# Gated unit of a fused attention, experts and gated-unit kernel: rows turned in squares of 32 on VectorE, sums of squares taken from the experts

## The chip, the cores and the metric

One NeuronCore of a Trainium2 chip runs the whole program. The metric is device time in microseconds (us). TensorE is called PE, VectorE DVE, ScalarE ACT, GpSimd POOL and SyncE SP, as in the profile; "the experts" is the expert layer, and "a product" is one MATMUL instruction.

## The reference, cut to what matters

Three layers follow each other. Only the last one and the rows that go into it matter here.

```python
x = _attn_ref(q, k, v)                      # 4608 rows of 512
out[mask] = gate_w[mask, None] * (np.maximum(xe @ w1[e], 0.0) @ w2[e])   # one expert of 8 per row
rms = np.sqrt(np.mean(x * x, axis=-1, keepdims=True) + 1e-06)            # gated unit, 512 -> 1536 -> 512
xn = x / rms * rms_g
g = xn @ w_gate
silu = g * (1.0 / (1.0 + np.exp(-g)))
return (silu * (xn @ w_val) @ w_out).astype(np.float32)
```

All numbers are float32; each float32 operand of a large product is split into a high and a low float32r part, so one product becomes three.

## The kernel before, in words

Attention runs first, in 36 tiles of 128 rows, and writes rows to DRAM (`x_d`). The expert layer runs in up to 25 slots of 256 rows that all belong to one expert. A slot gathers its rows, turns them on PE, multiplies with `w1` (`stage1`, L492 ff., eight steps f of 12 products with 256 columns; ACT takes the high part at L502 and DVE the low part at L503, and four PSUM tiles hold the results), then multiplies with `w2` (`stage2`, L927, two halves z of 128 rows, 24 products with 512 columns each). The result `y` lies in PSUM; ACT (z = 0, L943) or DVE (z = 1, L941) scales it with the gate into `ys`, and SP stores `ys` with one more column, the row's number, to `y_d` (L945). Half z = 1 stands under a branch (L973), since not each slot has more than 128 rows. While slots run, DVE, ACT and POOL also split the weights of the gated unit; 13 of its 18 units of weights are parked in DRAM (`scr`).

The gated unit (`NB` = 18 blocks kk of 256 rows, L1173 ff.) loads its rows with SP (`read_y`, L983), and the parked weights with POOL (`weights`, L1103). `norm` (L986) makes the steps of the normalisation: POOL copies the row numbers, ACT sums squares (L992), DVE finds 1/sqrt by Newton steps (L997 to L1007) and scales the rows (L1010). These steps are dealt out between the products of an earlier block, three behind each step c. `turn_y` (L1014) turns the rows, features to partitions, by eight transposes of 128x128 on PE (L1018); ACT takes the high part times the norm's weight (L1022) and DVE the low part (L1023). `gv(kk, c)` (L1130) is step c of 12: 24 products of 256 columns into one of three PSUM tiles `g` (L1137 to L1139), then tanh on ACT (L1141), two operations on DVE (L1142, L1143) and the split of the result into `ah`, `al` (L143, L144). `outp(kk)` (L1149) is the second multiplication: twice 36 products with 512 columns (L1158 to L1160), a copy by ACT and a scatter by POOL.

PE works in the order in which the code is written: output products of block kk-1, the eight turns for block kk+1, then the 288 products of block kk. Block 0 has its rows turned in the experts' last slot (`y0t`, in the pool of the weights); its own loop holds the turns for block 1, behind c = 9 and c = 10. The last block has no turns ahead of its products.

Tiles lie in pools in the order in which they are first asked for. The pool `g2` begins a multiple of 4096 bytes behind the first tile of the weights' pool, whose tiles all have 4096 bytes. In `g2` stand two `y` (1152 words each), two `o` (512 words) and two `gap` (8 words, L1168) ahead of `xh` and `xl`.

Of the kernel before, what the change touches and what calls it, by code (L numbers as in the profile page):

```python
# [21 lines left out]
NT = 4608  # L22
# [59 lines left out]
def fused(ctx: ExitStack, tc: tile.TileContext, q, k, v, moe_w_gate, moe_w1, moe_w2,  # L82
# [9 lines left out]
    y_d = dram.tile([NT + T, DM + 1], F32, name="y_d")  # L92
# [617 lines left out]
    nc.sync.dma_start(out=gt, in_=rms_g.rearrange("(k p o) -> p k o", p=128, o=1))  # L710
# [45 lines left out]
    ys = [mo.tile([128, DM + 1], F32, name=f"ys{i}") for i in range(2)]  # L756


    tid = sm1.tile([128, 1], I32, tag="tid", name="tid")
# [69 lines left out]
    def unit_src(u, j):  # L829
        if u < NC2:  # L830
            w = w_gate if j == 0 else w_val
            w = w.bitcast(I32) if wide else w
            n = 256 if wide else 128
            return w[:, u * n:u * n + n].rearrange("(k p) n -> p k n", p=128), 4
# [146 lines left out]
    ybl, toks = {}, {}  # L981

    def read_y(t, kk):  # L983
        nc.sync.dma_start(out=t, in_=y_d[kk * T:kk * T + T, :].rearrange("(z p) d -> p z d", p=128))

    def norm(y, tk, ms, yi, t, scratch):  # L986

        r = yi.bitcast(F32)
        steps = []

        def square(j):
            nc.scalar.activation(out=scratch(), in_=y[:, j, 0:DM], func=AF.Square, accum_out=ms[:, j:j + 1])  # L992

        steps.append(lambda: nc.gpsimd.tensor_copy(out=tk, in_=y[:, :, DM:DM + 1].bitcast(I32)))
        for j in range(2):
            steps.append(lambda j=j: square(j))
# [6 lines left out]
        for _ in range(3):  # L1003
            steps.append(lambda: nc.vector.tensor_tensor(out=t, in0=r, in1=r, op=ALU.mult))
            steps.append(lambda: nc.vector.scalar_tensor_tensor(out=t, in0=t, scalar=-0.5, in1=ms,
                                                                op0=ALU.mult, op1=ALU.mult))
            steps.append(lambda: nc.vector.scalar_tensor_tensor(out=r, in0=t, scalar=1.5, in1=r,  # L1007
                                                                op0=ALU.add, op1=ALU.mult))
        for j in range(2):
            steps.append(lambda j=j: nc.vector.tensor_scalar(  # L1010
                out=y[:, j, 0:DM], in0=y[:, j, 0:DM], scalar1=r[:, j:j + 1], scalar2=None, op0=ALU.mult))
        return steps

    def turn_y(y, to, c, px_):  # L1014
        hi, lo = to
        for d in range(2):
            for z in range(2):
                nc.tensor.transpose(px_[:, d, 128 * z:128 * z + 128],  # L1018
                                    y[:, z, (2 * c + d) * 128:(2 * c + d) * 128 + 128], ident)
# [83 lines left out]
    def weights(u):  # L1103
# [6 lines left out]
        else:  # L1110
            wo[u - NC2] = held[u]

    def load_y(kk):
# [3 lines left out]
    def norm_steps(kk):  # L1117
        toks[kk] = gs_p.tile([128, 2, 1], I32, tag="tk", bufs=3, name="tk")
        ms, yi, t = (gs_p.tile([128, 2], dt, tag=nm, name=nm) for dt, nm in ((F32, "ms"), (I32, "yi"), (F32, "t")))
        return norm(ybl[kk], toks[kk], ms, yi, t, lambda: g2.tile([128, DM], F32, tag="o", name="sq"))  # L1120

    def xpose2(kk, c):
        if c == 0:
            xts[kk] = (g2.tile([128, 4, T], F32R, tag="xh", name="xh"), g2.tile([128, 4, T], F32R, tag="xl", name="xl"))
        y = ybl[kk] if c == 0 else ybl.pop(kk)
        turn_y(y, xts[kk], c, pst.tile([128, 2, T], F32, tag=f"px{c}", name="px"))

    acts = {}

# [34 lines left out]
                in_=o, in_offset=None)  # L1164

    xts[0] = xts.pop("y0")
    load_y(1)
    g2.tile([128, 8], F32, tag="gap", name="gap")  # L1168
    for c in range(NC2):
        weights(c)  # L1170
    for c in range(6):
        weights(NC2 + c)
    for kk in range(NB):  # L1173


        todo = [] if kk else norm_steps(1)
        if kk:
            outp(kk - 1)
            if kk + 1 < NB:
                xpose2(kk + 1, 0)  # L1180
                xpose2(kk + 1, 1)
            if kk + 2 < NB:
                load_y(kk + 2)
                todo = norm_steps(kk + 2)
        for c in range(NC2):
            gv(kk, c)
            if kk:
                for f in todo[3 * (c - 5):3 * (c - 4)] if c > 4 else ():
                    f()
                continue  # L1190
            for f in todo[3 * (c - 2):3 * (c - 1)] if c > 1 else ():
                f()
            if c in (9, 10):
                xpose2(1, c - 9)
            if c == 8:
                load_y(2)
            if c == 11:
                for f in norm_steps(2):
                    f()
    outp(NB - 1)  # L1200


# [29 lines left out]
```

## Time and profile before

| | us |
|---|---|
| three runs, median (lowest to highest) | 1722.82 (1719.47 to 1733.78) |
| the profiled execution | 1731.15 |
| span of its instructions | 1729.1 |
| first to last product of the gated unit's first multiplication | 798.3 to 1705.9 |

The profiled execution is longer than the median and inside the spread of the runs. The profile's page gives the busy time of each engine; its views by window, by line, by time and by waits are cut to the rows below. A product in the time view begins where PE starts it; its written duration overlaps that of the next ones, so the distance of starts is what PE needs for one.

### The profile page before, as it was taken

What the parts mean: (1) busy time and instruction counts of PE and PEld (TensorE: products, weight loads), DVE (VectorE), ACT (ScalarE), POOL (GpSimd) and SP (SyncE); (2) the same over time, 40 slices, a digit from 0 to 9 for tenths busy, and PEclk for the clock granted to TensorE, in tenths of its full rate; (3) what the DMA queues carried; (4) which work ended last, traced back from release to release, by engine and by line L of the source; (5) the groups of instructions that cost most, each with busy time, mean ns of one, the idle gap of its engine ahead of it and who ended that gap; (6) DMA issues with size and microseconds to landing.
All of it is one profiled execution on the core that took longest, in us unless ns stands there. A gap on an engine that the chain in (4) does not pass through costs nothing.

```text
span 1729.1 us, 31214 instructions
## 1 busy us (share of the span) xinstructions
PE 1640.8 (95%) x11373; PEld 1507.4 (87%) x11373; DVE 883.4 (51%) x2087; ACT 527.8 (31%) x1202; POOL 425.9 (25%) x469
## 2 busy tenths in 40 slices
PE   7897888999899999998999999999999999999998
PEld 5897877878788888888899999999999999999997
DVE  5787875588866688423434433333433333443322
ACT  2344442244524244222222222222222222222221
POOL 4665564355534555212100000000000000000000
PEclk7798889999999999999999999999999999999999
DMA  9889665456754664214600000000000000000000
GB/s 183 220 167 189 127 110 157 132 194 226 258 191 148 200 210 142 75 51 169 217 10 19 23 26 25 25 26 7 20 25 25 25 25 7 20 26 13 13 13 13
DMA packets 111632, 162.16 MB, mean 94 GB/s; under 512 B 46032, under 2 KB 65616, under 8 KB 111456
## 3 DMA queue, kind: packets, MB, share of 16 engines
q1 hardware_dynamic: 99744, 124.03, 26.7%
q0 software_dynamic: 11712, 35.91, 6.1%
q8 instruction: 94, 1.54, 0.4%
q14 instruction: 82, 0.67, 0.1%
HBM read 116.85 MB, written 43.06 MB: 92 GB/s over the span
## 4 chain that ended last, share of the span: by engine, by line
PE 50%; DMA 2%; issue 1%; POOL 0%; POOLq 0%; ACT 0%
PE g L1138 11%; PE g L1139 11%; PE g L1137 11%; PE po L1159 6%; PE po L1160 6%; PE po L1158 6%; DMA rl<-scr 1%; PE px L1018 1%; DMA rh<-scr 1%; DMA out_dram<-o,tk 0%; POOL rh L1107 0%; POOL rl L1107 0%; POOLq L1226 0%; ACT o L1161 0%; POOLq L1107 0%
## 5 line engine op out<-in xcount | busy, mean ns | idle before, releaser
L1138 PE MATMUL g<-xl,rh 128*128 128x256 f32 x1088 | 302.8, 278 | 0.0
L1139 PE MATMUL g<-xh,rl 128*128 128x256 f32 x1088 | 302.7, 278 | 0.0
L1137 PE MATMUL g<-xh,rh 128*128 128x256 f32 x1088 | 302.4, 278 | 0.0
L1162 POOL DMA_INDIRECT out_dram<-o,tk x36 | 34.7, 965 | 793.9 <-ACT o L1161 708.4
L1138 PEld LDWEIGHTS g<-xl,rh 128*128 128x128 f32 x1088 | 204.3, 188 | 0.0
L1137 PEld LDWEIGHTS g<-xh,rh 128*128 128x128 f32 x1088 | 204.1, 188 | 0.0
L1139 PEld LDWEIGHTS g<-xh,rl 128*128 128x128 f32 x1088 | 204.0, 187 | 0.0
L498 PE MATMUL p<-xh,w1h 128*128 128x256 f32 x672 | 191.6, 285 | 7.7 <-DVE hl L503 7.1
L499 PE MATMUL p<-xl,w1h 128*128 128x256 f32 x672 | 190.0, 283 | 1.9 <-DVE xl L535 1.9
L500 PE MATMUL p<-xh,w1l 128*128 128x256 f32 x672 | 189.6, 282 | 0.0
L1142 DVE SCALAR_TENSOR_TENSOR th<-th,g 128x256 f32<-128x256 f32 x216 | 90.9, 421 | 191.8 <-ACT th L1141 191.3
L1023 DVE SCALAR_TENSOR_TENSOR xl<-px,gt,xh 128x256 fp32r<-128x256 f32 x68 | 31.4, 482 | 265.3 <-ACT xh L1022 265.3
L1137 PE MATMUL g<-xh,uh 128*128 128x256 f32 x544 | 152.6, 280 | 0.0
L1138 PE MATMUL g<-xl,uh 128*128 128x256 f32 x544 | 151.4, 278 | 0.0
L1139 PE MATMUL g<-xh,ul 128*128 128x256 f32 x544 | 151.4, 278 | 0.0
L143 ACT CAST ah<-th 128x256 fp32r<-128x256 f32 x216 | 88.0, 407 | 203.4 <-DVE th L1143 203.4
L1141 ACT ACTIVATE th<-g 128x256 f32<-128x256 f32 x216 | 82.6, 382 | 206.7 <-PE g L1139 206.6
L144 DVE TENSOR_TENSOR al<-th,ah 128x256 fp32r<-128x256 f32 x216 | 91.9, 425 | 102.2 <-ACT ah L143 102.2
L1159 PE MATMUL po<-rl,ah 128*128 128x512 f32 x360 | 142.4, 395 | 1.5 <-DMA rl<-scr 1.5
L1158 PE MATMUL po<-rh,ah 128*128 128x512 f32 x360 | 142.3, 395 | 0.0
L1160 PE MATMUL po<-rh,al 128*128 128x512 f32 x360 | 142.2, 395 | 0.0
L498 PEld LDWEIGHTS p<-xh,w1h 128*128 128x128 f32 x672 | 127.6, 190 | 12.3 <-DVE hl L503 8.3
(263 smaller groups left out, 3641.6 us busy)
## 6 DMA issues: line engine op xcount, KB each, us to landing
st<-in_moe_w_dram SPq DMA_DIRECT2D x64, 512.0 KB
y_d<-ys SPq DMA_DIRECT2D x39, 256.5 KB
y<-y_d SPq DMA_DIRECT2D x18, 513.0 KB
v<-in_v_dram SPq DMA_DIRECT2D x32, 288.0 KB
x_d<-x SPq DMA_DIRECT2D x32, 260.0 KB
q<-in_q_dram SPq DMA_DIRECT2D x32, 256.0 KB
scr<-uh SPq DMA_DIRECT2D x13, 512.0 KB
scr<-ul SPq DMA_DIRECT2D x13, 512.0 KB
```

Of the source, the lines that this page charges most:

```text
L143: nc.scalar.copy(out=hi, in_=src)
L144: eng.tensor_tensor(out=lo, in0=src, in1=hi, op=ALU.subtract)
L498: nc.tensor.matmul(a, lhsT=w1h[d][:, fs], rhs=xh[:, d], start=d == 0, stop=False)
L499: nc.tensor.matmul(a, lhsT=w1h[d][:, fs], rhs=xl[:, d], start=False, stop=False)
L500: nc.tensor.matmul(a, lhsT=w1l[d][:, fs], rhs=xh[:, d], start=False, stop=d == 3)
L1137: nc.tensor.matmul(g[:, j], lhsT=wh[:, sl], rhs=hi[:, d], start=d == 0, stop=False)
L1138: nc.tensor.matmul(g[:, j], lhsT=wh[:, sl], rhs=lo[:, d], start=False, stop=False)
L1139: nc.tensor.matmul(g[:, j], lhsT=wl[:, sl], rhs=hi[:, d], start=False, stop=d == 3)
L1142: nc.vector.scalar_tensor_tensor(out=th, in0=th, scalar=1.0, in1=g[:, 0], op0=ALU.add, op1=ALU.mult)
L1158: nc.tensor.matmul(po, lhsT=ah[:, tsl], rhs=wh[:, sl], start=c == 0, stop=False)
L1159: nc.tensor.matmul(po, lhsT=ah[:, tsl], rhs=wl[:, sl], start=False, stop=False)
L1160: nc.tensor.matmul(po, lhsT=al[:, tsl], rhs=wh[:, sl], start=False, stop=c == NC2 - 1)
```

## The change

Every row's sum of squares is taken in the experts: after `ys` is scaled, ACT squares `y` in place with the gate as scale and adds it up into a further column of `ys`; `y_d` gets that column. In the gated unit the rows of a block come in by four DMAs of 32 partitions (each 8 x 128 words per partition, so that squares of 32x32 lie where they are to be turned), their sums by four more and the row numbers by one. DVE scales the rows, turns them in two STREAM_TRANSPOSE instructions, and ACT and DVE split the result from SBUF. Features are numbered so that partition p holds features 4p to 4p+3; the loads of `w_gate`, `w_val` and `rms_g` and the turns of block 0 follow that. PE's eight turns go; one transpose of the constant identity stands in their place ahead of each block from 1 to 17. The tile `gap` goes and `y` has 1024 words; `yt` (one buffer of 1024 words) stands between `y` and `xh`.

```diff
+        nc.scalar.activation(out=y, in_=y, func=AF.Square, scale=g, accum_out=ys[z][:, DM + 1:DM + 2])
         r = nc.values_load(row_i[START:START + 1, s:s + 1], engines=(ET.SP,), min_val=0, max_val=NT)
         nc.sync.dma_start(out=y_d[bass.ds(r + 128 * z, 128), :], in_=ys[z])
...
     def load_y(kk):
-        ybl[kk] = g2.tile([128, 1152], F32, tag="y", name="y")[:, 0:2 * DM + 2].rearrange("p (z d) -> p z d", z=2)
-        read_y(ybl[kk], kk)
+        ybl[kk] = g2.tile([128, 8, 128], F32, tag="y", name="y")
+        sq[kk] = gs_p.tile([128, 8], F32, tag="sq", bufs=2, name="sq")
         toks[kk] = gs_p.tile([128, 2, 1], I32, tag="tk", bufs=3, name="tk")
+        rows = y_d[kk * T:kk * T + T, :]
+        for a in range(4):
+            ps_ = slice(32 * a, 32 * a + 32)
+            nc.sync.dma_start(out=ybl[kk][ps_], in_=rows[:, 128 * a:128 * a + 128].rearrange("(b i) d -> i b d", i=32))
+            nc.sync.dma_start(out=sq[kk][ps_].unsqueeze(2),
+                              in_=rows[:, DM + 1:DM + 2].rearrange("(b i) d -> i b d", i=32))
+        nc.sync.dma_start(out=toks[kk].bitcast(F32), in_=rows[:, DM:DM + 1].rearrange("(z p) d -> p z d", p=128))
+    def turn_steps(kk):
+        y, ms = ybl.pop(kk), sq.pop(kk)
+        steps = newton(ms, yi, t)
+        yt = g2.tile([128, 4, T], F32, tag="yt", bufs=1, name="yt")
+        xts[kk] = hi, lo = tuple(g2.tile([128, 4, T], F32R, tag=nm, name=nm) for nm in ("xh", "xl"))
+        def scale(h):
+            b = slice(4 * h, 4 * h + 4)
+            nc.vector.tensor_tensor(out=y[:, b], in0=y[:, b], in1=r[:, b].unsqueeze(2).to_broadcast([128, 4, 128]),
+                                    op=ALU.mult)
+        def turn(h):
+            c = slice(2 * h, 2 * h + 2)
+            nc.vector.transpose(out=yt[:, c].rearrange("p c (b i) -> p c b i", i=32),
+                                in_=y.rearrange("p b (j c) -> p c b j", c=4)[:, c])
+        def part(c):
+            nc.scalar.activation(out=hi[:, c], in_=yt[:, c], func=AF.Copy, scale=gt[:, c])
+            nc.vector.scalar_tensor_tensor(out=lo[:, c], in0=yt[:, c], scalar=gt[:, c], in1=hi[:, c],
+                                           op0=ALU.mult, op1=ALU.subtract)
+        return (steps + [lambda h=h: scale(h) for h in range(2)] + [lambda h=h: turn(h) for h in range(2)] +
+                [lambda c=c: part(c) for c in range(4)])
...
+    turned = pst.tile([128, 128], F32, tag="px", name="turned")
     load_y(1)
-    g2.tile([128, 8], F32, tag="gap", name="gap")
...
+        todo = turn_steps(kk + 1) if kk + 1 < NB else []
         if kk:
             outp(kk - 1)
-            if kk + 1 < NB:
-                xpose2(kk + 1, 0)
-                xpose2(kk + 1, 1)
-            if kk + 2 < NB:
-                load_y(kk + 2)
-                todo = norm_steps(kk + 2)
+            nc.tensor.transpose(turned, ident, ident)
+        if kk + 2 < NB:
+            load_y(kk + 2)
         for c in range(NC2):
             gv(kk, c)
+            for f in todo[2 * c:2 * c + 2] if kk else todo[3 * (c - 5):3 * (c - 4)] if c > 4 else ():
                 f()
```

On PE, between the output products (`po`) of block 0 and the products (`g`) of block 1, the kernel before has:

```order
L1160 MATMUL po<-uh_9334,al 128x512
L1018 MATMUL px<-cc,y 128x128 x8
L1137 MATMUL g<-xh,uh_2948 128x256
L1138 MATMUL g<-xl,uh_2948 128x256
L1139 MATMUL g<-xh,ul_2949 128x256
```

and the changed kernel has:

```order
L1196 MATMUL po<-uh_9368,al 128x512
L1215 MATMUL turned<-cc 128x128
L1173 MATMUL g<-xh,uh_2948 128x256
L1174 MATMUL g<-xl,uh_2948 128x256
L1175 MATMUL g<-xh,ul_2949 128x256
```

Eight turns of data have become one turn of constants (`cc`), and nothing else moved on PE at this place.

On SP, behind the store of the last slot (`ys` to `y_d`) and the ends of the slots' branches, the kernel before has the 17 loads of rows:

```order
L945 DMA y_d<-ys_2941 128x513
L973 UNCONDITIONAL_BRANCH x2
L1082 UNCONDITIONAL_BRANCH x7
L984 DMA y<-y_d 128x2x513 x17
```

and the changed kernel has nine for each block, of which the first block's stand here:

```order
L947 DMA y_d<-ys_2941 128x514
L975 UNCONDITIONAL_BRANCH x2
L1091 UNCONDITIONAL_BRANCH x7
L1133 DMA y<-y_d 32x8x128
L1134 DMA sq<-y_d 32x8x1
L1133 DMA y<-y_d 32x8x128
L1134 DMA sq<-y_d 32x8x1
L1133 DMA y<-y_d 32x8x128
L1134 DMA sq<-y_d 32x8x1
L1133 DMA y<-y_d 32x8x128
L1134 DMA sq<-y_d 32x8x1
L1136 DMA tk<-y_d 128x2x1
```

A load of 256 pieces has become nine loads of 2304 pieces: 1024 of 512 bytes and 1280 of 4 bytes.

On ACT, at the end of a slot of the experts (`ys_2940` belongs to the half z = 0, `ys_2941` to z = 1 inside its branch, `hh` to the next slot's first products), the changed kernel has:

```order
L944 ACTIVATE ys_2940<-y,gates 128x512
L945 ACTIVATE y,ys_2940<-y,gates 128x512
L883 CAST uh_4378<-ub 128x512
L907 TENSOR_LOAD row_i
L975 COMPARE_AND_BRANCH
L945 ACTIVATE y,ys_2941<-y,gates 128x512
L975 UNCONDITIONAL_BRANCH x2
L503 ACTIVATE hh<-p_0_3228 128x256
```

where the kernel before has

```order
L943 ACTIVATE ys_2940<-y,gates 128x512
L882 CAST uh_4370<-ub 128x512
L906 TENSOR_LOAD row_i
L973 COMPARE_AND_BRANCH
L973 UNCONDITIONAL_BRANCH x2
L502 ACTIVATE hh<-p_0_3226 128x256
```

Both squares are new; that of z = 1 stands ahead of the next slot's first `hh` and behind DVE's use of the same `y`.

## Rows read from the trace of the kernel before

**Rows 1.** Window of one block: length, PE, PEld, DVE, ACT, POOL busy (instructions), granted clock, DMA, GB/s.
```profile
1570.20:1621.80 51.60, 51.60 (x370) 48.29 (x369) 19.43 (x54) 13.48 (x34) 2.11 (x3) 1.00 0.03 11
```

**Rows 2.** Time view of PE: last output product and first two products, around eight turns.
```profile
1569.87 0.40 PE L1160 MATMUL po<-uh,al 128*128 128x512 f32 x1
...
1570.90 0.36 PE L1137 MATMUL g<-xh,uh 128*128 128x256 f32 x1
1571.10 0.28 PE L1138 MATMUL g<-xl,uh 128*128 128x256 f32 x1
```

**Rows 3.** Time view of PE: the same at block 17, which has no turns.
```profile
1671.78 0.39 PE L1160 MATMUL po<-uh,al 128*128 128x512 f32 x1
1672.01 0.28 PE L1137 MATMUL g<-xh,uh 128*128 128x256 f32 x1
1672.12 0.28 PE L1138 MATMUL g<-xl,uh 128*128 128x256 f32 x1
```

**Rows 4.** Chain that ended last: turns ahead of blocks 1, 10, 11 and 12.
```profile
854.33 0.87 PE px L1018 x8
...
1314.85 0.87 PE px L1018 x8
1365.16 0.87 PE px L1018 x8
...
1416.76 0.87 PE px L1018 x8
```

**Rows 5.** Time view of PE: block 10, block 17: its 288 products' start or end.
```profile
1315.48 0.36 PE L1137 MATMUL g<-xh,uh 128*128 128x256 f32 x1
...
1348.20 0.39 PE L1158 MATMUL po<-rh,ah 128*128 128x512 f32 x1
...
1705.93 0.40 PE L1158 MATMUL po<-rh,ah 128*128 128x512 f32 x1
```

**Rows 6.** Time view of PE: block 0, first product of c = 2 and turns behind c = 9.
```profile
805.49 0.28 PE L1137 MATMUL g<-y0t,uh 128*128 128x256 f32 x1
...
828.53 0.60 PE L1018 MATMUL px<-cc,y 128*128 128x128 f32 x4
```

**Rows 7.** Time view of PE: experts' slot 0, two products twelve apart.
```profile
260.18 0.28 PE L499 MATMUL p<-xt,w1h 128*128 128x256 f32 x1
...
261.62 0.28 PE L499 MATMUL p<-xt,w1h 128*128 128x256 f32 x1
```

**Rows 8.** Groups by line on DVE and ACT: busy, mean ns | idle before, releaser.
```profile
L426 DVE TENSOR_TENSOR x<-av,rs 128x512 f32<-128x512 f32 x35 | 23.8, 680 | 0.0
...
L992 ACT ACTIVATION_READ_ACCUMULATOR sq<-y 128x1 f32 x36 | 6.7, 187 | 0.0
L943 ACT ACTIVATE ys<-y,gates 128x512 f32<-128x512 f32 x22 | 15.1, 686 | 32.8 <-PE y L935 22.8 <-PEq L973 3.6 <-ACTq L910 2.5
L941 DVE TENSOR_SCALAR ys<-y,gates 128x512 f32<-128x512 f32 x17 | 12.7, 748 | 42.8 <-PE y L935 41.7 <-DMA st<-in_moe_w_dram 1.1
```

**Rows 9.** Time view of all engines at the end of a slot of the experts.
```profile
602.94 0.75 DVE L941 TENSOR_SCALAR ys<-y,gates 128x512 f32<-128x512 f32 x1 [4.06 <-PE y L935]
...
604.42 0.38 ACT L502 ACTIVATE hh<-p 128x256 fp32r<-128x256 f32 x1 [5.84 <-PE p L500]
...
606.26 0.42 DVE L503 SCALAR_TENSOR_TENSOR hl<-p,hh 128x256 fp32r<-128x256 f32 x1 [0.99 <-ACT hh L502]
```

**Rows 10.** DMA queues in 804:812 (two), 14:17 and 84.3:84.7: packets, MB, share of 16 engines.
```profile
q0 software_dynamic: 498, 1.84, 64.1%
q1 hardware_dynamic: 544, 1.05, 40.2%
...
q1 hardware_dynamic: 1607, 0.57, 100.5%
...
q0 software_dynamic: 28, 0.00, 5.1%
```

**Rows 11.** Chain that ended last: the last parked weights.
```profile
836.00 7.05 DMA rl<-scr
```

More of the change, by code (lines that the diff above doesn't have):

```diff
@@ L91, in fused @@
     x_d = dram.tile([NT, XW], F32, name="x_d")
-    y_d = dram.tile([NT + T, DM + 1], F32, name="y_d")
+    y_d = dram.tile([NT + T, DM + 2], F32, name="y_d")
     ord_d = dram.tile([E * NT, 1], I32, name="ord_d")
@@ L709, in fused @@
     nc.sync.dma_start(out=ct, in_=cst[:, C_TRI:C_END])
-    nc.sync.dma_start(out=gt, in_=rms_g.rearrange("(k p o) -> p k o", p=128, o=1))
+    nc.sync.dma_start(out=gt, in_=rms_g.rearrange("(p k o) -> p k o", k=4, o=1))
     nc.sync.dma_start(out=ord_d.rearrange("(p n) o -> p (n o)", p=128), in_=bigt)
@@ L755, in fused @@
     xgs = [mo.tile([128, 2, XW], F32, name=f"xg{i}") for i in range(2)]
-    ys = [mo.tile([128, DM + 1], F32, name=f"ys{i}") for i in range(2)]
+    ys = [mo.tile([128, DM + 2], F32, name=f"ys{i}") for i in range(2)]
     tid = sm1.tile([128, 1], I32, tag="tid", name="tid")
@@ L833, in unit_src @@
             n = 256 if wide else 128
-            return w[:, u * n:u * n + n].rearrange("(k p) n -> p k n", p=128), 4
+            return w[:, u * n:u * n + n].rearrange("(p k) n -> p k n", k=4), 4
         w = w_out.bitcast(I32) if wide else w_out
@@ L983, in read_y, with newton @@
     def read_y(t, kk):
-        nc.sync.dma_start(out=t, in_=y_d[kk * T:kk * T + T, :].rearrange("(z p) d -> p z d", p=128))
-    def norm(y, tk, ms, yi, t, scratch):
+        nc.sync.dma_start(out=t, in_=y_d[kk * T:kk * T + T, 0:DM + 1].rearrange("(z p) d -> p z d", p=128))
+    def newton(ms, yi, t):
         r = yi.bitcast(F32)
         steps = []
[L991 to L996, printed above, removed]
         steps.append(lambda: nc.vector.tensor_scalar(out=ms, in0=ms, scalar1=1.0 / DM, scalar2=1e-6,
@@ L1008, in norm, with square @@
                                                                 op0=ALU.add, op1=ALU.mult))
+        return steps
+    def norm(y, tk, ms, yi, t, scratch):
+        steps = []
+        def square(j):
+            nc.scalar.activation(out=scratch(), in_=y[:, j, 0:DM], func=AF.Square, accum_out=ms[:, j:j + 1])
+        steps.append(lambda: nc.gpsimd.tensor_copy(out=tk, in_=y[:, :, DM:DM + 1].bitcast(I32)))
+        for j in range(2):
+            steps.append(lambda j=j: square(j))
+        steps += newton(ms, yi, t)
+        r = yi.bitcast(F32)
         for j in range(2):
@@ L1018, in turn_y @@
                 nc.tensor.transpose(px_[:, d, 128 * z:128 * z + 128],
-                                    y[:, z, (2 * c + d) * 128:(2 * c + d) * 128 + 128], ident)
+                                    y[:, z, 2 * c + d:DM:4], ident)
         for d in range(2):
@@ L1111, in weights @@
             wo[u - NC2] = held[u]
+    sq = {}
     def load_y(kk):
-        ybl[kk] = g2.tile([128, 1152], F32, tag="y", name="y")[:, 0:2 * DM + 2].rearrange("p (z d) -> p z d", z=2)
-        read_y(ybl[kk], kk)
-    def norm_steps(kk):
+        ybl[kk] = g2.tile([128, 8, 128], F32, tag="y", name="y")
+        sq[kk] = gs_p.tile([128, 8], F32, tag="sq", bufs=2, name="sq")
         toks[kk] = gs_p.tile([128, 2, 1], I32, tag="tk", bufs=3, name="tk")
-        ms, yi, t = (gs_p.tile([128, 2], dt, tag=nm, name=nm) for dt, nm in ((F32, "ms"), (I32, "yi"), (F32, "t")))
-        return norm(ybl[kk], toks[kk], ms, yi, t, lambda: g2.tile([128, DM], F32, tag="o", name="sq"))
@@ L1122, in xpose2 @@
[L1122 to L1126, printed above, removed]
+        rows = y_d[kk * T:kk * T + T, :]
[4 more added lines that the diff above has]
+                              in_=rows[:, DM + 1:DM + 2].rearrange("(b i) d -> i b d", i=32))
@@ new lines, in load_y @@
+        nc.sync.dma_start(out=toks[kk].bitcast(F32), in_=rows[:, DM:DM + 1].rearrange("(z p) d -> p z d", p=128))
+    def turn_steps(kk):
+        y, ms = ybl.pop(kk), sq.pop(kk)
+        yi, t = (gs_p.tile([128, 8], dt, tag=nm, name=nm) for dt, nm in ((I32, "yi"), (F32, "t")))
+        steps = newton(ms, yi, t)
+        r = yi.bitcast(F32)
+        yt = g2.tile([128, 4, T], F32, tag="yt", bufs=1, name="yt")
[14 more added lines that the diff above has]
+                [lambda c=c: part(c) for c in range(4)])
@@ L1173, in fused @@
     for kk in range(NB):
-        todo = [] if kk else norm_steps(1)
+        todo = turn_steps(kk + 1) if kk + 1 < NB else []
         if kk:
             outp(kk - 1)
-            if kk + 1 < NB:
-                xpose2(kk + 1, 0)
-                xpose2(kk + 1, 1)
-            if kk + 2 < NB:
-                load_y(kk + 2)
-                todo = norm_steps(kk + 2)
+            nc.tensor.transpose(turned, ident, ident)
+        if kk + 2 < NB:
+            load_y(kk + 2)
         for c in range(NC2):
             gv(kk, c)
[L1187 to L1191, printed above, removed]
-                f()
[L1193 to L1199, printed above, removed]
+            for f in todo[2 * c:2 * c + 2] if kk else todo[3 * (c - 5):3 * (c - 4)] if c > 4 else ():
+                f()
     outp(NB - 1)
```

## The prediction, made before the changed kernel had run

> **What bounds the kernel now.** I looked at the window view by stage first, then at the time view of PE, then at what shares the other engines and the DMA queues. From block 1 to the end PE works without a gap: in one block of 51.60 us its busy time is 51.60, while DVE has 19.43 and ACT 13.48 [rows 1], at the full 2.4 GHz (granted clock 1.00). So in this half of the program only what PE itself starts costs time; work that moves to DVE or ACT is free as long as no wait for it reaches PE. In a block PE starts 288 products of 256 columns, 72 output products of 512 and eight turns.
>
> The reader should see next that blocks differ. The turns ahead of blocks 10, 11 and 12 begin 50.31 and 51.60 us apart; from block 1 to block 10 it is 460.52, three times 50.31 + 51.60 + 51.60 within 0.01 [rows 4]. So every third block (1, 4, ... 16) is 1.29 us shorter. Block 10, a short one, takes 32.72 us for its 288 products, 113.6 ns each [rows 5]; a long block then takes 32.72 + 1.29 = 34.01, 118 ns each; block 17 takes 1705.93 - 1672.01 = 33.92, the long kind, and is the one block with no turns ahead of it [rows 3, 5]. Block 0 is a third kind: 192 products in 23.04 us, 120.0 ns each [rows 6]. The experts' slot 0 has the same 120.0 (twelve products in 1.44 us) [rows 7]. Nothing waits in any of these: PE's own rhythm differs by 6%, and with 17 blocks of 288 products that is more time than the turns themselves.
>
> **The turns on PE.** With eight turns the distance from the last output product to the second product is 1571.10 - 1569.87 = 1.23 us [rows 2]; with none it is 1672.12 - 1671.78 = 0.34 [rows 3]. Eight turns so cost 0.89, one about 0.11, and one is left: 0.78 saved for each of blocks 1 to 16, less 0.11 for block 17, which gains a turn: 16 x 0.78 - 0.11 = 12.4 us. Block 0 loses its own eight turns, 0.9 us, but behind block 0 PE waits for the last parked weights, which land at 843.05 [rows 11]; I count nothing for them.
>
> **The place of the moving operand.** The two tiles that are read at 120.0 ns (`y0t`, `xt`) lie in the weights' pool. In pool `g2`, `xh` stands 2 x 4608 + 2 x 2048 + 2 x 32 = 13,376 bytes behind the pool's beginning, 64 bytes past a multiple of 512; the beginning itself is a multiple of 4096 bytes from every weight tile and from `y0t` and `xt`. After the change `y` takes 2 x 4096 and `yt` 4096, `gap` is gone, and `xh` and `xl` stand at multiples of 4096 from `y0t`. So every block's moving operand gets the place that in this trace always ran at 120.0 ns, at several starts: straight, behind four turns of block 0, and in slot 0 of the experts. That the place is the cause is my reading of three cases that agree, not something the trace isolates. By it a block's products take 288 x 0.1200 + 0.08 (the first one behind a turn) = 34.64 us: 1.92 more in six short blocks, 0.63 more in ten long ones, 0.72 in block 17, together 11.5 + 6.3 + 0.7 = 18.5 us lost. The bounds from the nearest rows are the other two rhythms: all 17 blocks at 32.72 would give back 10 x 1.29 + 1.20 = 14.1; all at 34.01 would lose 6 x 1.29 = 7.7. I take +18.5, the row with the same place.
>
> The Trainium skill says otherwise: in "TensorE: Matmul & The Clock Gate", "Step-by-step: what each phase is for", the gap between products in a stream is the number of columns in cycles plus about 2.5 ns, by which 256 columns would take about 109 ns (an estimate from that page) wherever they lie. The trace has 113.6, 118 and 120.0, so here the rule gives a floor and no single rhythm; by it this term would be 0.
>
> **DVE and ACT in a block.** Two turns by DVE are shown by no row. The nearest of 512 elements are L426's 680 ns and L941's 748 [rows 8]; between none and three times the latter a pair costs 0 to 4.5 us, and I take 1.4. The scaling with a broadcast operand is priced as L426: 2 x 0.68. DVE's 19.43 us becomes about 22, ACT loses two squares. All lies beside 50 us of PE. Three `g` tiles give two steps of c (5.7 us) before a late DVE stops PE, so even 4.5 costs nothing.
>
> **Experts.** A square is priced as L943's 686 ns from the same PSUM tile plus 187 for reading the sum: 0.87 us, 22 + 17 times [rows 8], 34 us of ACT. For z = 0 it lies beside the other half's 24 products. For z = 1 it waits for DVE: DVE ends at 603.69, the square at about 604.6, where ACT took the next `hh` at 604.42; behind it DVE idled 0.99 us [rows 9], which absorbs 0.2 to 0.5. SP's store comes 0.9 later at a point where only later slots' loads queue behind it. Bounds: nothing, and 17 x 0.5 = 8 us; no gain, since work is only added. I take 1, near the idle row.
>
> **The first block's loads.** Both loads of rows run beside the parked weights. A packet of 2052 bytes took 0.402 x 16 x 8 us / 544 = 95 ns; packets of mostly 256 bytes 1.005 x 16 x 3 / 1607 = 30 ns; packets of 4 bytes 0.051 x 16 x 0.4 / 28 = 12 ns [rows 10]. A load becomes 1024 x 0.037 (an estimate between 30 and 95, nearer the first) + 1280 x 0.012 = 53 us over 16 engines, 3.3 us, against 256 x 0.095 / 16 = 1.5. Two loads add 3.6 us to a stream whose end PE waits for [rows 11]. I take 3; bounds 0 (if they fit ahead of the weights) and 8 (below).
>
> **Sum.** -12.4 + 18.5 + 1 + 3 = +10.1 us. The profiled execution would go from 1731.15 to 1741; it lies 8.3 above the median of the runs, so from that median of 1722.8 I forecast 1733.
>
> **Rivals.**
> 1. The one turn puts every block in the short rhythm. For it: only blocks behind turns ever had it, and block 17 did not. Against it: block 0 has turns in its middle and stays at 120.0 on both sides. -12.4 - 14.1 + 4 = -22.5: 1700.
> 2. The rhythms stay as a mix (-12.4 + 4: 1714), or all blocks have the long one (-12.4 + 7.7 + 4: 1722), because the place is not the cause. For it: 118 ns is the commonest kind.
> 3. Slower: DVE is held in block 0. Its first Newton step stands behind step c = 5 and needs the four loads of sums, the last of which is eighth in SP's row; DVE's work for c = 6 is queued behind it. PE fills three `g` tiles and must stop at 828.53 - 2.88 = 825.65. DVE then needs 1.4 us to free one, so this decides from a landing later than 824.2 on. In the shared window the two queues passed 498 and 544 packets, about one for one [rows 10]. One for one with 4096-byte packets, 2048 small ones last 128 per engine x 0.2 = 26 us from 804, to 830 to 832. PE stops for 6 to 8 us instead of 3 for this term: forecast + 5, and 8 more if the weights behind slip too: 1738 to 1746. The Trainium skill bears on it: "DMA: Bandwidth & Descriptors", "Queues, rings and completion order", says that each engine takes turns between queues packet by packet, and that a packet can hold many descriptors; by the latter the small ones would pass faster than I count, and 498 to 544 agrees with the first half of the rule only.
>
> **How the numbers follow.** Chances: forecast 0.42 (own range 1726 to 1741), rival 1 0.28, rival 2 0.18, rival 3 0.12. A measurement of this kernel tells about 1%, 17 us, from no change: faster means under 1706, slower over 1740. Faster: nine tenths of rival 1 and a little of rival 2, 0.26. Slower: rival 3 (0.12) and 0.03 of the forecast's case, 0.15. The rest, 0.59, is no change. Cases of both signs hold the chance, so the range runs from rival 1's 1700 less 1 to 1743, the middle of rival 3.
>
> **What would show it.** Right: 288 products of a block in 34.6 us in all blocks; 0.46 us from the last output product to the second product; DVE near 22 us in a block with no PE idle; PE's wait for `rl` behind block 0 a few us longer. Wrong: any block at 32.7 or 34.0 (the place is not the cause), PE idle in block 0 with DVE at its first Newton step (rival 3), PE idle at slot ends behind ACT's square.

## The result, and the profile after

The changed kernel took 1735.68 us (median of 20 runs, 1727.78 to 1747.33), the kernel before 1724.42 beside it (20 runs, 1719.47 to 1733.78). The ratio is 1.0058, with a 95% interval from 1.0042 to 1.0073: a little slower, by less than the 1% from which the prediction's chances count a change. The forecast was 1733.

The profiled execution took 1731.95 us and its span is 1730.1, against 1731.15 and 1729.1 before. The two spans are 1 us apart and the medians 11, so the spans must not be subtracted. The attention and the experts ahead of the gated unit took anything from 789 to 809 us in the profiled executions of this study, whatever the edit. I therefore count each trace from block 0's first product:

| | before | after | difference |
|---|---|---|---|
| first product of block 0 | 798.26 | 789.25 | (spread of executions) |
| from there to block 1's first product | 56.70 | 67.07 | +10.4 |
| from there to the last output product | 867.54 | 867.19 | -0.4 |

All of the loss lies in block 0, and the 17 blocks behind it come out even. The window view shows block 0 of the kernel before; its columns are those of [rows 1]:

```profile
798.26:854.96 56.70, 55.19 (x377) 51.01 (x377) 22.27 (x68) 14.72 (x39) 15.19 (x29) 0.97 0.79 274
```

and block 0 and a later block of the kernel after:

```profile
789.25:856.29 67.04, 58.67 (x360) 54.13 (x361) 21.44 (x56) 11.38 (x29) 14.93 (x27) 0.87 1.14 232
...
1570.81:1621.84 51.03, 51.03 (x364) 48.15 (x363) 21.30 (x56) 12.06 (x30) 1.92 (x2) 1.00 0.03 11
```

In the later block PE is busy for the whole 51.03 us at full clock, as in [rows 1], and DVE's time went from 19.43 to 21.30. In block 0 PE is idle for 8.4 us (1.5 before), and the granted clock is 0.87 (0.97 before): part of it runs at the lower of the clock's two levels.

The time view of PE in a later block answers to [rows 2, 3, 5]:

```profile
1570.43 0.40 PE L1196 MATMUL po<-uh,al 128*128 128x512 f32 x1
1570.66 0.27 PE L1215 MATMUL turned<-cc 128*128 128x128 f32 x1
1570.69 0.36 PE L1173 MATMUL g<-xh,uh 128*128 128x256 f32 x1
1570.89 0.28 PE L1174 MATMUL g<-xl,uh 128*128 128x256 f32 x1
...
1605.33 0.40 PE L1194 MATMUL po<-rh,ah 128*128 128x512 f32 x1
...
1621.45 0.40 PE L1196 MATMUL po<-uh,al 128*128 128x512 f32 x1
```

Three things are to be read. From the last output product to the second product it is 0.46 us (1.23 before). The 288 products take 1605.33 - 1570.69 = 34.64 us, 120.0 ns each, and so they do in all 17 blocks. And the 72 output products take 1621.45 - 1605.33 = 16.12 us from the first to the last start, 227 ns each; before it was 16.56, 233 ns each: in block 10 from 1348.20 [rows 5] to

```profile
1364.76 0.40 PE L1160 MATMUL po<-uh,al 128*128 128x512 f32 x1
```

This third one I had not looked at.

The groups by line on DVE and ACT, the columns those of [rows 8]:

```profile
L1153 DVE STREAM_TRANSPOSE yt<-y 128x512 f32<-128x512 f32 x34 | 36.4, 1107 | 0.0
L1148 DVE TENSOR_TENSOR y<-y,yi 128x512 f32<-128x512 f32 x34 | 21.9, 684 | 0.0
L992 DVE TENSOR_SCALAR sq<-sq 128x8 f32<-128x8 f32 x17 | 2.8, 165 | 9.4 <-DMA sq<-y_d 9.4
...
L945 ACT ACTIVATE y<-y,gates 128x512 f32<-128x512 f32 x39 | 25.6, 656 | 55.2 <-issue 28.7 <-DVE ys L942 24.0 <-DMA st<-in_moe_w_dram 2.5
```

A turn of 512 elements per partition takes DVE 1107 ns; a pair is 2.2 us (I took 1.4, bounds 0 to 4.5). L992 is the first Newton step: over all 17 blocks DVE waited 9.4 us for the sums, and the time views of DVE and of PE show that all of it stands in block 0:

```profile
810.50 0.42 DVE L145 TENSOR_TENSOR al<-th,ah 128x256 fp32r<-128x256 f32 x1 [0.47 <-ACT ah L144]
820.29 0.17 DVE L992 TENSOR_SCALAR sq<-sq 128x8 f32<-128x8 f32 x1 [9.36 <-DMA sq<-y_d]
...
821.23 0.42 DVE L1179 SCALAR_TENSOR_TENSOR th<-th,g 128x256 f32<-128x256 f32 x1
```

```profile
816.99 0.28 PE L1175 MATMUL g<-y0t,rl 128*128 128x256 f32 x1
821.70 0.58 PE L1173 MATMUL g<-y0t,rh 128*128 128x256 f32 x1 [4.43 <-DVE th L1179]
822.08 0.42 PE L1174 MATMUL g<-y0t,rh 128*128 128x256 f32 x1
```

DVE is held from 810.93 to 820.29 by the landing of the sums. PE fills its three `g` tiles, starts its last product at 816.99 and goes on at 821.70, when the first tile comes free: 4.6 us lost. Then it runs at the lower clock for a while, as the window view of the stop and of the stretch behind it shows:

```profile
816.99:821.70 4.71, 0.28 (x3) 0.08 (x2) 1.26 (x5) 0.02 (x1) 1.59 (x3) 0.90 1.75 362
821.70:827.62 5.92, 5.92 (x27) 5.92 (x28) 4.01 (x16) 2.09 (x6) 1.06 (x2) 0.50 1.64 350
```

27 products take 5.92 us at a granted clock of 0.50, the 1.2 GHz level, where 27 x 0.12 is 3.24: 2.7 us more, 7.3 in all.

Why the sums come late: the eight loads of rows and sums of block 1 are issued by SP from 794.00 on, and in the window 794 to 820 the DMA queues passed, by packets, MB and share of 16 engines:

```profile
q0 software_dynamic: 2162, 7.91, 97.1%
q1 hardware_dynamic: 2337, 0.53, 57.7%
```

q0 has the parked weights, q1 the rows: one packet for one, and some 2300 packets, one block's load, need 26 us. From 800 to 833, in each single microsecond, the numbers of packets that the two queues begin lie within 6 of each other (72 to 107 each).

The chain that ended last, in block 0 (start, us, what), answers to [rows 11]:

```profile
812.74 12.36 DMA rh<-scr
825.15 8.19 issue
833.35 0.47 POOL rh L1116
833.87 9.29 DMA rl<-scr
843.20 0.80 PE po L1195
844.00 0.43 PE po L1196
```

At 825.15 the last pair of parked weights waits for the tile it is to go into. It is the one of `y0t`, and POOL's wait ends with the last product of block 0 ("PE g L1175" in the time view of POOL). So block 0's products set when that pair is issued, and the pair sets when the output products of block 0 can be finished. Counted from block 0's first product, the last load is issued after 44.6 us (before: 37.7), lands after 53.9 (44.8), and block 1 starts after 67.1 (56.7). The 10.4 us are thus 6.9 of a later issue (DVE's hold, passed on), 2.2 of a longer transfer and 1.3 behind it, where output products run at the lower clock for 5 us (843.2 to 848.2: granted clock 0.51, 0.43 us apart; 1.00 in the kernel before) and the eight turns are gone.

### The profile page after: what moved, and what is told of

Same layout as the page of the kernel before. It is cut to its first block, busy times and chain, and to the rows that moved or that the text cites. A ratio compares the mean times of both kernels' runs of the same rounds, so it can differ in the third digit from the quotient of the medians.

```text
span 1730.1 us, 31209 instructions
## 1 busy us (share of the span) xinstructions
PE 1634.9 (94%) x11253; PEld 1508.3 (87%) x11254; DVE 916.5 (53%) x2121; ACT 529.0 (31%) x1212; POOL 423.8 (24%) x452
## 4 chain that ended last, share of the span: by engine, by line
PE 50%; DMA 2%; issue 1%; POOL 0%; POOLq 0%; ACT 0%
PE g L1175 11%; PE g L1174 11%; PE g L1173 11%; PE po L1195 5%; PE po L1196 5%; PE po L1194 5%; DMA rl<-scr 1%; DMA rh<-scr 1%; DMA out_dram<-o,tk 0%; POOL rh L1116 0%; PE turned L1215 0%; POOL rl L1116 0%; POOLq L1248 0%; ACT o L1197 0%; POOLq L1116 0%
## 5 line engine op out<-in xcount | busy, mean ns | idle before, releaser
L1173 PE MATMUL g<-xh,rh 128*128 128x256 f32 x1088 | 307.9, 283 | 0.0
L1174 PE MATMUL g<-xl,rh 128*128 128x256 f32 x1088 | 307.9, 283 | 0.0
L1175 PE MATMUL g<-xh,rl 128*128 128x256 f32 x1088 | 307.9, 283 | 0.0
L1173 PEld LDWEIGHTS g<-xh,rh 128*128 128x128 f32 x1088 | 208.9, 192 | 0.0
L1174 PEld LDWEIGHTS g<-xl,rh 128*128 128x128 f32 x1088 | 208.9, 192 | 0.0
L1175 PEld LDWEIGHTS g<-xh,rl 128*128 128x128 f32 x1088 | 208.9, 192 | 0.0
L1175 PE MATMUL g<-xh,ul 128*128 128x256 f32 x544 | 154.0, 283 | 0.0
L500 PEld LDWEIGHTS p<-xl,w1h 128*128 128x128 f32 x672 | 129.4, 193 | 2.5 <-DVE xl L536 1.8
```

Of the source, the lines that this page charges most:

```text
L500: nc.tensor.matmul(a, lhsT=w1h[d][:, fs], rhs=xl[:, d], start=False, stop=False)
L1173: nc.tensor.matmul(g[:, j], lhsT=wh[:, sl], rhs=hi[:, d], start=d == 0, stop=False)
L1174: nc.tensor.matmul(g[:, j], lhsT=wh[:, sl], rhs=lo[:, d], start=False, stop=False)
L1175: nc.tensor.matmul(g[:, j], lhsT=wl[:, sl], rhs=hi[:, d], start=False, stop=d == 3)
```

## The experiments

Byte places below are those of the tiles in a partition, in the compiled program, modulo 512. All weight tiles, `y0t` among them, stand at 448. The kernels ran in groups, each group on one chip beside the kernel before, whose median differs by up to 8 us from group to group; so I compare ratios to it.

**e1_gap: the gap put back.** `xh`, `xl`, `ah` and `al` stand at 0 again, as before the change, and nothing else differs.

```diff
     load_y(1)
+    g2.tile([128, 8], F32, tag="gap", name="gap")
```

> The changed kernel with the 64 bytes of the old gap put back ahead of yt, xh, xl, o, ah and al; all else as changed. Place theory (where the moving operand lies sets the distance of products): no block from 1 to 17 stays at 120.0 ns; they go to 113.3 or 117.8, and output products, whose stationary operand moves by 64 bytes too, go from about 226.5 back to 233.3 ns. Time against the changed kernel: 17 blocks lose between 0.63 and 1.92 us of products and gain 0.48 us of output products, so -2.5 to -24 us. Rival (the turns between output and next products set the distance, not the place): 120.0 ns stays and the time is that of the changed kernel, 1736, within 2.

Measured: ratio 1.0057 (1.0030 to 1.0083). In its trace all 17 blocks have 117.8 ns a product, 34.01 us, and output products take 16.57 us again:

```profile
1318.33 0.36 PE L1173 MATMUL g<-xh,uh 128*128 128x256 f32 x1
...
1352.33 0.39 PE L1194 MATMUL po<-rh,ah 128*128 128x512 f32 x1
...
1368.90 0.39 PE L1196 MATMUL po<-uh,al 128*128 128x512 f32 x1
```

So the place moves both rhythms, in opposite directions: 0.63 us won and 0.45 lost per block, 3 us in 17 blocks, which is too little for the ratio to show. The short rhythm of 113.3 does not come with one turn at this place.

**e2_before_nogap: the kernel before without its gap**, with eight turns of data as ever.

```diff
     load_y(1)
-    g2.tile([128, 8], F32, tag="gap", name="gap")
```

> The kernel before with its gap of 64 bytes taken out and nothing else changed, so eight turns of data stand between output and next products. Place theory: all blocks at 120.0 ns, block period 34.56 + 0.9 of turns + 72 output products; +18.5 us of products, and -8 us if output products go to 226.5 ns because ah moves by the same 64 bytes: 1724 + 10 = 1735. Rival (turns set the distance): mix of 113.3 and 117.8 stays, time 1724 within 2.

Measured: 1.0100 (1.0054 to 1.0147; four runs). All 17 blocks are at 120.0 ns, their outputs at 16.12 us. Block 10 takes 34.64 us:

```profile
1316.77 0.36 PE L1137 MATMUL g<-xh,uh 128*128 128x256 f32 x1
...
1351.41 0.40 PE L1158 MATMUL po<-rh,ah 128*128 128x512 f32 x1
```

The mix of 113.3 and 117.8 is gone although turns, squares and loads are those of the kernel before. The 64 bytes alone make the 120.0; that it is the place of `xh` and `xl` and not of `ah` and `al` is for the next run to show.

**e3_swap_gap: the two places apart.** Pool `ga` stands ahead of `g2`, so `ah` keeps 448 while the gap brings `xh` to 0.

```diff
-    g2 = gctx.enter_context(tc.tile_pool(name="g2", bufs=2))
     ga = gctx.enter_context(tc.tile_pool(name="ga", bufs=13))
+    g2 = gctx.enter_context(tc.tile_pool(name="g2", bufs=2))
...
     load_y(1)
+    g2.tile([128, 8], F32, tag="gap", name="gap")
```

> As e1_gap, but the pool of ah and al stands ahead of that of y, yt, xh and xl, so only xh and xl (and yt, o) move by 64 bytes and ah, al keep the place mod 512 of the changed kernel. If the two places act one by one: products as in e1_gap (113.3 or 117.8 ns) and output products at about 226.5 ns, 17 x 0.48 = 8 us less than e1_gap. If it is one place for both (the sum of all that moves): the same as e1_gap.

Measured: 1.0002 (0.9977 to 1.0026). The two places act one by one: 34.01 us for the products and 16.12 for the outputs in every block. In the time view of block 10:

```profile
1317.94 0.36 PE L1173 MATMUL g<-xh,uh 128*128 128x256 f32 x1
...
1351.95 0.39 PE L1194 MATMUL po<-rh,ah 128*128 128x512 f32 x1
...
1368.07 0.40 PE L1196 MATMUL po<-uh,al 128*128 128x512 f32 x1
```

**e4_noturn: no turn of constants.**

```diff
-    turned = pst.tile([128, 128], F32, tag="px", name="turned")
...
-            nc.tensor.transpose(turned, ident, ident)
```

> The changed kernel without the one turn of constants. If the turn only costs what it takes: 17 x 0.11 to 0.2 us less, -2 to -3.5 us, products stay at 120.0 ns. Rival (the turn sets the rhythm): the distance of products changes from 120.0 ns, and the time by several us either way.

Measured: 1.0052 (1.0025 to 1.0080). 120.0 ns stay; a block's period is 50.90 us instead of 51.03. At place 448 the turn sets no rhythm and costs 0.13 us per block, 2.2 in all.

**e5_late0: block 1's steps later**, so that DVE does not wait for the sums ahead of block 0's own work.

```diff
-            for f in todo[2 * c:2 * c + 2] if kk else todo[3 * (c - 5):3 * (c - 4)] if c > 4 else ():
+            for f in todo[2 * c:2 * c + 2] if kk else todo if c == 11 else ():
```

> The changed kernel with one edit: in block 0 all of block 1's steps (Newton, scaling, turns, splits) stand behind step c = 11 instead of three behind each step from c = 5 on. Theory (DVE's hold): in the changed kernel's trace PE stops 7.3 us at c = 8 to 10 of block 0, because DVE waits 9.4 us for the sums and the g tiles fill; the last parked weights wait for block 0's last products (their tile is the one of y0t), so the hold is passed on whole. With the edit block 0 takes 34.6 us for its 288 products instead of 41.9, the last parked weights are issued some 37 us behind block 0's first product instead of 44, and block 1 begins 58 to 60 us behind it instead of 67: 7 to 9 us off the time, 1725 to 1729. Rival (the transfer sets the end): the parked weights, slowed by the small packets of the rows' loads, land as late as before, PE waits at the output products for what it no longer waits for in the products: gain 0 to 2 us, 1733 to 1736. Second rival (the late steps become late themselves): block 1 waits for its xh, gain lost.

Measured: 1.0044 (1.0009 to 1.0078); the changed kernel's 1.0058 lies inside this interval. The trace says more. Block 0's products take 37.34 us instead of 43.75 and no wait for DVE is left among them; the last load is issued 38.2 us behind the first product instead of 44.6; but it then takes longer:

```profile
844.24 2.56 issue
...
847.33 11.83 DMA rl<-scr
```

11.83 us instead of 9.29, and block 1 starts after 62.5 us instead of 67.1. The first two expectations each had a part: the hold is removed, 6.4 us, and 2.5 are given back to the transfer. What runs beside it is seen in the queues: between 847 and 859 q1 still passed 2396 packets, the rows of block 2 and, issued by SP from 854.67 on, those of block 3.

**e7_late0_y1: as e5, with one `y` tile**, so that the rows of blocks 2 and 3 cannot be loaded beside the parked weights.

```diff
-        ybl[kk] = g2.tile([128, 8, 128], F32, tag="y", name="y")
+        ybl[kk] = g2.tile([128, 8, 128], F32, tag="y", bufs=1, name="y")
```

> As the kernel with block 1's steps behind c = 11, and one y tile instead of two, so that the load of rows for block 2 waits until block 1's rows are turned, and every later load likewise: one load of 2304 pieces, not two, shares block 0's time with the parked weights. xh, xl, ah and al keep their places mod 512 bytes. If the small pieces slow the weights: the parked weights that are issued early pass faster (the issues of the 13 pairs end some 2 to 3 us earlier against block 0's first product), the last pair lands 7 us behind its issue instead of 9.3, and the time is 1 to 3 us under that of the kernel with two y tiles. If it is the products of block 0 that hold the last pair: the same time within 1 us. Against both, one y tile could make a later block wait for its rows: then PE idles in blocks 1 to 16 and the time is over 1736.

Measured: 1.0004 (0.9979 to 1.0029).

```profile
843.41 8.74 DMA rl<-scr
```

The last load takes 8.74 us (I had expected 7), block 1 starts 56.9 us behind block 0's first product (56.7 in the kernel before), and no later block waits for its rows. The 5.6 us won against e5 are more than the 1 to 3 that I expected: 3.1 are the transfer, 0.9 its earlier issue, and 1.6 the output products behind it, which here run at full clock from the landing on (granted clock 1.00 from 852.2 to 863.0). While the last weights land (843 to 852), the queues passed

```profile
q0 software_dynamic: 855, 3.10, 98.4%
q1 hardware_dynamic: 37, 0.02, 3.1%
```

where in the changed kernel (834 to 843, SP issuing the rows of block 3 from 834.54 on) they had passed

```profile
q1 hardware_dynamic: 2952, 0.64, 68.1%
q0 software_dynamic: 324, 1.15, 64.4%
```

e5 and e7 move like amounts of weights (852 and 855 packets of q0), so the 3.1 us between their transfers are the small packets' price; in the changed kernel only 324 packets of weights were left, since the hold had let the earlier pairs land, and they took 9.29 us all the same. That accounts for block 0: a hold of DVE by the small packets of block 1's rows, and a slower last transfer by those of blocks 2 and 3.

**e6_square2: the experts' squares doubled**, to price their term.

```diff
+        nc.scalar.activation(out=y, in_=y, func=AF.Copy, accum_out=ys[z][:, DM + 1:DM + 2])
         nc.scalar.activation(out=y, in_=y, func=AF.Square, scale=g, accum_out=ys[z][:, DM + 1:DM + 2])
```

> The changed kernel with a second pass of ACT over y (a copy in place with a sum, 0.66 + 0.19 us) ahead of each square in the experts, so the added work on ACT is doubled: 22 + 17 times 0.85 us, 33 us of ACT. Theory (the predicted idle time hides the square): one square per half fits into slack, since the spans of the experts are alike without and with it (first to last scaling of the second half 488.3 us before, 485.8 after); of the second, the half under the branch stands between DVE's scaling and the next slot's first hh, and 0.5 to 0.85 us per slot come through in up to 17 slots: 8 to 14 us in the experts' span, 1744 to 1750. Rival (ACT in the experts is far off PE's path, so squares cost nothing at any number): 1733 to 1738 with the experts' span unchanged. Rival (the first square already costs its 0.5 per slot and something else hid it): the second costs its whole 0.85 x 17 = 14 us.

Measured: 1.0058 (1.0037 to 1.0078), the ratio of the changed kernel itself. The theory fell: 39 more passes of 0.59 + 0.19 us, 30 us of ACT, cost nothing that can be measured (the interval is some 3.5 us to either side). From the first to the last scaling of a second half the experts take 491.7 us; traces with one square have 483.2 to 491.6, the two without (the kernel before and e2) 488.3 and 488.7. In the slot end that I followed, ACT's passes end at 582.6; ACT has two `hh` ready at once behind them and then waits 0.81 us for PE, so the delay is caught up in the next slot's first steps.

**e8_eight: as e3_swap_gap, with eight turns of constants.**

```diff
-            nc.tensor.transpose(turned, ident, ident)
+            for _ in range(8):
+                nc.tensor.transpose(turned, ident, ident)
```

> The changed kernel with pool ga ahead of g2 and a tile of 64 bytes, so that xh stands at a multiple of 512 bytes and ah 64 bytes ahead of one, and eight turns of the constant identity ahead of each block instead of one. The same with one turn took 1725.8 with all blocks at 117.8 ns a product. If the turns set the rhythm at this place: every third block (or every block) goes at 113.6 ns, 1.29 us less in 6 blocks (or 1.2 in 17), and seven more turns cost 7 x 0.11 x 17 = 13 us: 1731 (or 1718). If what they move matters (data from y, with ACT and DVE taking px), not their number: all blocks at 117.8 and 13 us more, 1738 to 1740.

Measured: 1.0077 (1.0036 to 1.0118), 0.0075 above e3_swap_gap, 12.9 us: seven turns more in 17 blocks at 0.11 each. All blocks stay at 117.8. Eight turns alone do not bring back the short rhythm of the kernel before.

**e9_scan_a and e10_scan_b: other places and numbers of turns.** On top of e3, e5 and e7, `xh` and `xl` of odd and of even blocks have places of their own, and the number of turns changes every four blocks. The gap has 32 words in e9 and 48 in e10.

```diff
+        if kk == 2:
+            g2.tile([128, 32], F32, tag="gap2", bufs=1, name="gap2")
-        xts[kk] = hi, lo = tuple(g2.tile([128, 4, T], F32R, tag=nm, name=nm) for nm in ("xh", "xl"))
+        xts[kk] = hi, lo = tuple(g2.tile([128, 4, T], F32R, tag=f"{nm}{kk % 2}", bufs=1, name=f"{nm}{kk % 2}")
+                                 for nm in ("xh", "xl"))
...
+    g2.tile([128, 32], F32, tag="gap", bufs=1, name="gap")
...
-            nc.tensor.transpose(turned, ident, ident)
+            for _ in range((1, 8, 0, 3)[min((kk - 1) // 4, 3)]):
+                nc.tensor.transpose(turned, ident, ident)
```

> Pool ga ahead of g2, one y tile, block 1's steps behind c = 11, as in the kernel of the same call without a scan; and the moving operand of blocks of odd number at 64 mod 512 bytes, of even number at 192, with 1, 8, 0 and 3 turns of constants ahead of blocks 1 to 4, 5 to 8, 9 to 12 and 13 to 17. So far 448 mod 512 (the weights' own) gave 120.0 ns a product, 0 gave 117.8 or 113.3. Theory (place alone): each parity has one rhythm in all its blocks, whatever the turns; 64 and 192, being off the weights' place, have 117.8 or 113.3. Rival (the number of turns chooses between 113.3 and 117.8 where the place is off the weights'): the rhythm changes at blocks 5, 9 or 13, in both parities. Second rival (only the weights' place is special): 117.8 in all 17 blocks.

> The same with odd blocks at 128 and even blocks at 256 mod 512 bytes. Theory (place alone): one rhythm for each parity. Rival (turns): a change at blocks 5, 9 or 13. Second rival: 117.8 in all 17 blocks.

Measured, one run each: 1731.45 and 1719.16 us, where the kernel before had 1732.26. The reading is the rhythm of each block. With those of the other runs (ns per product):

| place of `xh`, `xl` | behind 1 or 8 turns | behind 0 or 3 turns |
|---|---|---|
| 0 (e1, e3, e8, e11) | 117.8 | 117.8 (0 turns: block 17 of the kernel before) |
| 64 (odd blocks of e9) | 118.7 | 120.0 |
| 128 (odd blocks of e10; e12) | 113.3 | 117.8 |
| 192 (even blocks of e9) | 120.0 | 120.0 |
| 256 (even blocks of e10) | 117.8 | 117.8 |
| 448 (after, e2, e4) | 120.0 | 120.0 (0 turns) |

The theory that only the weights' place is special fell, and so did that of the place alone: at 128 the number of turns chooses (and not the block's number: e12 below has one turn ahead of blocks 9 to 17 too, and 113.3 in them). In the time view of e10_scan_b, block 5 (eight turns) and block 9 (none), first product and first output product of each:

```profile
1055.69 0.37 PE L1176 MATMUL g<-xh,uh 128*128 128x256 f32 x1
...
1088.42 0.39 PE L1197 MATMUL po<-rh,ah 128*128 128x512 f32 x1
...
1256.94 0.28 PE L1176 MATMUL g<-xh,uh 128*128 128x256 f32 x1
...
1290.86 0.39 PE L1197 MATMUL po<-rh,ah 128*128 128x512 f32 x1
```

32.73 us against 33.92, in blocks with the same tiles at the same place.

**e11_best1: what the runs gave, together**: e3's order of pools and gap, e5's late steps, e7's one `y` tile.

> The changed kernel with what the runs so far gave: pool ga ahead of g2 and a tile of 64 bytes (xh at 0 mod 512, ah at the weights' place), one y tile, block 1's steps behind c = 11. From its own terms: 17 blocks with 288 products at 117.8 instead of 120.0 ns, 10.7 us less, and block 0 with 57 us instead of 67 to the start of block 1, 10 us less; the changed kernel stood 1.0058 of the kernel before, so 1.0058 - 20.7 / 1725 = 0.994. If the two edits hide each other (they are at different blocks, so they should not): 0.997 to 1.000.

Measured: 1718.05 us, 0.9918 (0.9893 to 0.9944). The two edits add up: in its trace blocks 1 to 17 take 10.8 us less than in the changed kernel and block 0 takes 9.7 less. It is faster than the kernel before and the changed one.

**e12_all128: the same with `xh`, `xl` at 128 in all blocks.**

```diff
-    g2.tile([128, 8], F32, tag="gap", name="gap")
+    g2.tile([128, 48], F32, tag="gap", bufs=1, name="gap")
```

> As e11_best1, which took 0.9918 of the kernel before with all blocks at 117.8 ns a product and xh at 0 mod 512 bytes; here xh and xl stand at 128 mod 512 in all blocks, with one turn of constants. In the scan, odd blocks at 128 ran at 113.3 with one turn or eight, and at 117.8 with none or three, each behind an even block at 256. If a block's rhythm follows from its own place and the number of turns: 113.3 in all 17 blocks, 1.28 us less in each, 21.8 us, 0.979. If it follows from the point in PE's rhythm at which the block ahead left off as well: some blocks at 113.3 (a third, as in the kernel before, would give 0.987; half 0.985), or none (0.992).

Measured: 1697.0 us, 0.9803 (0.9759 to 0.9846), the lowest ratio of all. All 17 blocks run at 113.3 ns with one turn, while block 0, whose `y0t` stays at 448, keeps its 120.0; the time view and the window of block 10:

```profile
1296.05 0.37 PE L1173 MATMUL g<-xh,uh 128*128 128x256 f32 x1
1296.25 0.28 PE L1174 MATMUL g<-xl,uh 128*128 128x256 f32 x1
...
1328.79 0.39 PE L1194 MATMUL po<-rh,ah 128*128 128x512 f32 x1
```

```profile
1296.05:1345.16 49.11, 49.11 (x364) 46.23 (x362) 21.23 (x56) 12.05 (x30) 1.92 (x2) 1.00 0.09 23
```

The block's period is 49.11 us, where e11 had 50.39 and the changed kernel 51.03.

## Why the prediction was right, and where it was not

The time came out 3 us from the forecast and inside what I had called no change, the likeliest outcome (0.59). The cause that I had named for most of the loss is shown, but the sum got there with two errors that cancel, and that they cancel is luck.

- **The turns on PE**, -12.4: right. 0.46 us from the last output product to the second product, as foretold, so 0.77 saved in 16 blocks and 0.12 spent in block 17: -12.2. e4 prices the remaining turn at 0.13 us, I had 0.11.
- **The place of the moving operand**, +18.5: right in size (34.64 us in every block, 18.5 more over 17 blocks) and in cause. I had called it my reading of three cases; e1 and e2 show it, by giving the gap to one kernel and taking it from the other, and e3 shows that it is `xh` and `xl`. The Trainium skill's rule ("TensorE: Matmul & The Clock Gate", "Step-by-step: what each phase is for": columns in cycles and about 2.5 ns, so some 109 ns for 256 columns, an estimate from that page) stayed a floor that no block reached; the nearest is 113.3, at place 128 and in the short blocks of the kernel before.
- **The output products**: the step that was missing. My part on the place spoke of `xh` alone, but pool `ga` lies behind `g2`, and `ah` and `al` moved by the same 64 bytes, to a place at which an output product takes 227 ns instead of 233. 17 blocks of 16.12 instead of 16.56 us are -7.5, a term that I had put at nothing. e3 shows the two effects apart. I had counted the 72 output products and never asked what their operands' places do.
- **The first block's loads**, "I take 3; bounds 0 (if they fit ahead of the weights) and 8": mis-sized; it measures 11 (10.4 net of the turns ahead of block 1), outside my bounds. What I described as rival 3, with a chance of 0.12, took place: the sums landed 26.3 us behind their first issue (26 there), PE stopped, and the weights behind slipped too. The rival had 6 to 8 us of stop; a stop of 4.6 and 2.7 at the lower clock were measured. Its 0.2 us for a pair of packets, which no row gave, measures 0.18 (26 us x 16 engines / 2337). I weighed its queue model (one packet for one) too low against my estimate by packet durations, 53 us over 16 engines, 3.3 us for a load. Beside the weights the packets of q1 take 0.577 x 16 x 26 = 240 us of the engines' time from 794 to 820, and the load lands after 26 us. The Trainium skill states such turns ("DMA: Bandwidth & Descriptors", "Queues, rings and completion order": each engine goes from queue to queue packet by packet); 2162 to 2337 packets agree with that.
- **Experts**, +1 (0 to 8): nothing that shows, by e6 even at twice the work.
- **DVE and ACT in a block**, free: right. DVE has 21.30 us (22 foretold) and PE no idle time in blocks 1 to 17.

The sum with what was measured is -12.2 + 18.5 - 7.5 + 11.1 + 0 = +9.9, against +10.1 foretold, +10.0 in the two traces from block 0 on and +11.3 between the medians.

Of the rivals, the first (one turn puts every block in the short rhythm) is false at this place, where the number of turns changes nothing, but its mechanism exists: at 128 one turn makes all blocks short (e12) and none makes them long (e10). The second, that the place is not the cause, is refuted. With place 128 in the changed kernel its 17 blocks would take 17 x (34.64 - 32.74) = 32 us less, about 1703 (an estimate; no run has that edit alone), and rival 1's 1700 would have been the better forecast.

## What to carry to other kernels

When an edit changes the size of any tile, list which operands of the busiest engine's stream move, stationary ones too, and look at the distance of starts in each kind of block: here 64 bytes cost 18.5 us in one kind of product and gave back 7.5 in the other, where the turns that the edit removed were worth 12. A load that is cut into small pieces should be counted in packets against the packets it shares engines with, not in bytes or in its own packets' time; and where a load must be cut so, its first use belongs behind the work of the engine that would wait for it, and its next one out of the way of the transfer that sets the end.

## What the runs showed that I had not expected

The rhythm of a stream of float32r products with nothing to wait for took a few fixed values in the gated unit (113.3, 117.8, 118.7 and 120.0 ns for 256 columns; 227 and 233 for 512). It depends on the operands' places: among the six places tried, all multiples of 64 bytes, 0, 128 and 256 gave 113.3 or 117.8, and 64, 192 and 448 gave 118.7 or 120.0. At 64 and 128 it also depends on how many turns stand ahead of the stream. A block keeps its rhythm over all 288 products.

The experts hold a seventh place that I had not read, in the kernel before too. From slot 1 on their `xh` and `xl` stand at 160, with weights at 448, and where nothing waits a product takes 118.3 ns. In the kernel after, the first and last of 96 products:

```profile
476.85 0.28 PE L499 MATMUL p<-xh,w1h 128*128 128x256 f32 x1
...
488.09 0.28 PE L501 MATMUL p<-xh,w1l 128*128 128x256 f32 x1
```

Open: whether the places count by themselves or against that of the weights, which stood at 448 in every kernel; why one and eight turns go together, and none and three; and why in the kernel before every third block was short, since eight turns of constants with `xh` at the same place (e8, with `ah` elsewhere) never brought that back. A run with the weights moved, and one with eight turns of data ahead of each block of the changed kernel, would tell more; neither was made.
